# Keys and queries from two PSUM banks instead of three, the second product accumulated on a copy of the first

## The chip, the cores and the metric

The kernel runs on one core of one Trainium2 chip. The metric is the device time of one execution in microseconds (us); lower is better. The engines that matter are PE (the tensor engine, matmuls), ACT (the scalar engine), DVE (the vector engine), POOL, and SP, which issues most DMAs. Each engine works through its own list of instructions in order and waits at semaphores for the others.

## The reference

The input x has 2048 rows of 512 numbers. Cut to what matters:

```python
xn = layernorm(x)                                  # per row, eps 1e-5
# A: linear attention, 32 heads of 16
q, k, v = heads(xn @ wqkv)                         # per head, 2048 x 16
phi = lambda t: where(t > 0, t + 1, exp(t)) + 1e-6
num = phi(q) @ (phi(k).T @ v)
den = phi(q) @ phi(k).sum(rows) + 1e-6
s = concat_heads(num / den) @ wo
# B: token-mixing block, then an MLP
h  = gelu(layernorm(xn) @ w1)
x1 = xn + shift_rows(h, quarters of the columns by +1, -1, +2, -2) @ w2
g  = silu(x1 + gelu(layernorm(x1) @ w3) @ w4)      # 512 -> 1376 -> 512
out = x + s * g
```

## The kernel before

The 2048 rows are 16 tiles of 128, numbered 0 to 15, in four blocks of four tiles. A product of fp32 accuracy is made as three matmuls (`products`): each operand is split into a rounded high part and a low part, and high·high, high·low and low·high are added up in PSUM. A matmul of the kind that matters here is 128x512. The names in the profile and the order are those of the tiles with the buffer's number left out; `wk_0h` is the high part of a piece of the key weights, `u_0l` the low part of a piece of the rows.

PSUM holds eight banks: four of the pool `acc` (in the first part of the program they hold the Gram sums `g`), and four of the pool `mm`, which everything else takes in turn.

Keys and queries of block 0 are made directly (`k`, `q`; `qsum` is a row of column sums of the query weights, made from `wqmh`, which ACT rounds from `wqt`). For blocks 1 to 3 they are made by a scheme of seven products for a 2x2 block matrix: the left matrix is two row tiles (i and k = i+2) by two halves of the columns, the right one the key weights and the query weights by two halves of the rows. Seven products of sums replace eight. The sums of the rows are `U[b]` (a11, a12, a22, s1 to s4; in the trace `u` and `us`), those of the weights `TW` (b11, b21, b22, t1 to t4; in the trace `wk`, `kq`, `wq`). One call of `keys_queries(b, j)` makes the keys and queries of two tiles with 42 matmuls, six for each product. There are six calls, (1,0) to (3,1), with i = 4, 5, 8, 9, 12, 13.

In a call, PSUM banks `pbk`, `pek`, `pak` take the products; ACT copies a bank to SBUF with `pl.act(..., AF.Copy)`; DVE adds with `pl.tt(..., ALU.add)`. The key of tile i is a11·b11 + a12·b21: the first product stands in `pbk`, ACT copies it to `p1k`, the second is made in a bank of its own, `pak`, and DVE adds the two. The other three results need the running sums a11·b11 + s2·t2 (copied to `u2k`) and s1·t1 (copied to `p5k`). `feature_k` then applies phi with two ACT instructions (`kr`, `kt`) and goes on with DVE; `feature_q(i, t)` of these blocks stores the query t.

Behind this stage come `mix1`/`mix2` (tiles `h`, `pbm`, `pam`, `pem`), and from about 214 us on the MLP and the output of the attention of all four blocks (`a`, `pb`, `pe`, `pa`, `uc`, `pbs`, `pes`, `pas`). The last two groups of the program are the two column halves of tile 15, banks `a` and `a4x`, handled by `gate` (L1479). For `a`, DVE first adds a held part (`e<-a,e`), ACT applies silu (`th<-e`), DVE multiplies (`th<-th,so`) and adds x (`th<-th,xr`), and the result is stored. For `a4x` the held part is added by the tensor engine, and ACT reads the bank directly (`th<-a4x`).

What sets the order: the code only lists operations. `Plan.emit` is a list scheduler that walks time forward with modelled durations and picks on each engine the ready operation that is due first; a matmul that is later in the list may be drawn ahead to fill. A table of pairs, `SOONER` (an operation's number, and by how many quarters of a microsecond it is due sooner), nudges the due times by hand. The numbers count operations, so they shift when the code has more or fewer of them. On each engine the resulting list is then fixed.

Of the kernel before, what the change touches and what calls it, by code (L numbers as in the profile page):

```python
# [430 lines left out]
def linear_attn_gated_by_mixer(  # L431
# [479 lines left out]

    def keys_queries(b, j):

        i, k = b * QT + j, b * QT + j + 2
        pa, pb, pe = (bank(f"{n}k{i}") for n in ("pa", "pb", "pe"))
        p1, p5, u2 = (piece(f"{n}k{i}") for n in ("p1", "p5", "u2"))

        def go(ps, x, y, start=True):
            products(ps, [both(U[b][x][c], j * P, (j + 1) * P) + TW[y][c] for c in range(2)], start, more=not start)

        go(pb, "a11", "b11")
        pl.act(p1, pb, AF.Copy)
        go(pe, "s1", "t1")
        pl.act(p5, pe, AF.Copy)
        go(pb, "s2", "t2", False)
        pl.act(u2, pb, AF.Copy)
        go(pa, "a12", "b21")
        pl.tt(p1, pa, p1, ALU.add)
        go(pb, "s3", "t3", False)
        pl.tt(p5, pb, p5, ALU.add)  # L930
        go(pe, "s4", "b22", False)
        pl.tt(u2, u2, pe, ALU.add)
        feature_k(i, p1, True)
        go(pb, "a22", "t4", False)
        feature_k(k, pb, True)
        feature_q(i, u2)
        feature_q(k, p5)
# [727 lines left out]
    for b in range(NQ):  # L1665
# [138 lines left out]
```

## Time and profile before

| | |
|---|---|
| median of 3 runs | 503.85 us (503.77 to 504.27) |
| profiled execution | 503.29 us |
| its span | 501.5 us |
| granted clock, mean | 0.999 |

The span runs from the first to the last instruction on the core; 1.8 us of the time lie around it. The page gives busy shares per engine, the trace each instruction's start and duration. A matmul's duration (0.39 us for 128x512) is longer than the distance of two starts (0.23 us), since matmuls are pipelined.

| queue or engine | rows before |
|---|---|
| PE | 3102 instructions, 494.1 us busy |
| ACT | 859, 387.4 us |
| DVE | 944, 443.4 us |
| POOL | 97, 82.7 us |

### The profile page before, as it was taken

The numbers are of one execution on the slowest core, as the hardware profiler recorded it, in microseconds if no ns is written. First come the engines' busy times: TensorE is split into PE (matmuls) and PEld (weight loads), VectorE is DVE, ScalarE is ACT, GpSimd is POOL, SyncE is SP. The second block draws the span as 40 slices with busy tenths as digits, with TensorE's granted clock in tenths as the row PEclk, the third lists the DMA queues.
The fourth block names the chain that finished last, engine by engine and source line by source line (L and its number), as shares of the span: only waits on it lengthen the run. The fifth ranks groups of instructions, "written<-read, shape, count | busy, mean of one in ns | idle before, by whom it ended". The sixth has DMA issues, their size and how long they took to land.

```text
span 501.5 us, 9471 instructions
## 1 busy us (share of the span) xinstructions
PE 494.1 (99%) x3102; PEld 442.1 (88%) x3102; DVE 443.4 (88%) x944; ACT 387.4 (77%) x859; POOL 82.7 (16%) x97
## 2 busy tenths in 40 slices
PE   8999999999999999999999999999999999999996
PEld 6777887898888888899899999999899998999995
DVE  6899999999699896999999998998899979987364
ACT  6899799766888795977767688957799778977451
POOL 1267123131221022020100011200020200201101
PEclk9999999999999999999999999999999999999999
DMA  7959984479976799989776698988598886896805
GB/s 254 337 138 256 321 256 128 99 157 279 335 219 160 219 307 214 288 232 330 256 250 214 218 326 229 267 255 241 192 275 277 226 207 216 283 329 189 200 1 126
DMA packets 86989, 116.69 MB, mean 233 GB/s; under 512 B 8864, under 2 KB 41148, under 8 KB 86940
## 3 DMA queue, kind: packets, MB, share of 16 engines
q1 hardware_dynamic: 77004, 98.00, 60.2%
q0 software_dynamic: 9936, 18.09, 20.9%
q8 instruction: 24, 0.39, 0.3%
q14 instruction: 25, 0.20, 0.1%
HBM read 73.70 MB, written 32.91 MB: 213 GB/s over the span
## 4 chain that ended last, share of the span: by engine, by line
PE 90%; ACT 4%; DMA 3%; DVE 1%; SPq 0%; issue 0%; ACTq 0%
PE a L151 14%; PE pb L151 10%; PE h L151 9%; PE g L151 9%; PE pbk L151 7%; PE acc L151 6%; PE pe L151 5%; PE pbm L151 5%; PE pbs L151 5%; PE pek L151 3%; PE uc L151 3%; PE pa L151 2%; PE pes L151 2%; PE pem L151 2%; PE pak L151 2%; PE q L151 1%
## 5 line engine op out<-in xcount | busy, mean ns | idle before, releaser
L230 POOL DMA_DIRECT2D th<-in_x x14 | 12.3, 930 | 166.3 <-DMA w_t<-w4t 75.3
L230 POOL DMA_DIRECT2D o<-x x16 | 13.8, 866 | 63.9 <-DVE o L198 42.7
L178 ACT ACT_TABLE_LOAD x18 | 23.1, 1283 | 0.3
L230 POOL DMA_DIRECT2D zacc<-kr x16 | 16.9, 1058 | 35.6 <-DVE kr L208 16.8
L173 ACT ACTIVATE gf<-gf 128x256 f32<-128x256 f32 (+1 forms) x48 | 21.9, 468 | 0.3
L652 POOL TENSOR_TENSOR rs<-w,nhalf 128x4 f32<-128x4 f32 (+2 forms) x10 | 15.8, 1643 | 36.8 <-DVE w L203 36.8
L230 POOL DMA_DIRECT2D e<-x1d x12 | 10.6, 1083 | 63.3 <-DVE e L198 59.7
L173 ACT ACT_TABLE_LOAD x11 | 14.1, 1283 | 2.2 <-issue 1.0
L173 ACT ACTIVATE ht<-ht 128x512 f32<-128x512 f32 x16 | 9.8, 625 | 6.7 <-DVE ht L198 6.2
L208 DVE SCALAR_TENSOR_TENSOR kr<-kt,kr 128x512 f32<-128x512 f32 x16 | 10.9, 684 | 4.3 <-ACT kt L173 4.2
L198 DVE TENSOR_TENSOR th<-th,so 128x512 f32<-128x512 f32 (+1 forms) x17 | 11.0, 655 | 3.6 <-ACT th L173 3.6
L198 DVE TENSOR_TENSOR e<-a,e 128x512 f32<-128x512 f32 (+1 forms) x17 | 9.8, 588 | 4.8 <-PE a L151 4.8
L173 ACT ACTIVATE y<-o,nm,rs 128x512 f32<-128x512 f32 x16 | 11.8, 806 | 2.6 <-DVE nm L208 2.6
L646 DVE BATCH_NORM_STATS2 st<-o 128x6 f32<-128x512 f32 x16 | 10.8, 686 | 3.3 <-DMA o<-x 3.3
L173 ACT ACTIVATE p<-pe 128x256 f32<-128x256 f32 x20 | 7.6, 382 | 7.4 <-PE pe L151 7.4
L198 DVE TENSOR_TENSOR gf<-pa,p 128x256 f32<-128x256 f32 x20 | 8.4, 422 | 5.1 <-PE pa L151 4.5
L173 ACT ACTIVATE x<-x,nm,rs 128x512 f32<-128x512 f32 x16 | 12.9, 804 | 0.0
L173 ACT ACTIVATE th<-e 128x512 f32<-128x512 f32 (+1 forms) x12 | 7.1, 606 | 7.5 <-DVE e L198 7.4
L198 DVE TENSOR_TENSOR ht<-h,abc 128x512 f32<-128x512 f32 x16 | 10.9, 686 | 1.2 <-PE h L151 1.0
L173 ACT ACTIVATE p<-pb 128x256 f32<-128x256 f32 x20 | 7.5, 377 | 5.4 <-PE pb L151 5.3
L208 DVE SCALAR_TENSOR_TENSOR pq<-pq,rd 128x512 f32<-128x512 f32 x16 | 10.9, 678 | 0.1
L1413 DVE TENSOR_REDUCE den<-qz 128x32 f32<-128x512 f32 x16 | 10.8, 681 | 0.1
(1868 smaller groups left out, 2288.5 us busy)
## 6 DMA issues: line engine op xcount, KB each, us to landing
w_s<-in_w SPq DMA_DIRECT2D x34, 256.0 KB, 5.1
w_t<-w4t SPq DMA_DIRECT2D x26, 256.0 KB, 6.2
w_b<-w4d SPq DMA_DIRECT2D x24, 256.0 KB, 4.7
x<-in_x SPq DMA_DIRECT2D x16, 256.0 KB, 6.2
zacc<-kr POOLq DMA_DIRECT2D x16, 256.0 KB, 4.9
o<-x POOLq DMA_DIRECT2D x16, 256.0 KB, 4.7
x1d<-o SPq DMA_DIRECT2D x16, 256.0 KB, 3.2
xt<-in_xt SPq DMA_DIRECT2D x15, 256.0 KB, 6.3
```

Of the source, the lines that this page charges most:

```text
L151: lambda: nc.tensor.matmul(out.get(), lhs.get(), rhs.get(), start=start, stop=stop, skip_group_check=more))
L173: nc.scalar.activation(out.get(), src.get(), func, scale=get(scale), **kw)
L178: op.warm = lambda: nc.scalar.activation(self.scr[1].get(), self.scr[0].get(), func)
L198: self.vec(eng, out, [a, b], lambda: self.e(eng).tensor_tensor(out.get(), a.get(), b.get(), op=op), True)
L208: lambda: self.nc.vector.scalar_tensor_tensor(out.get(), a.get(), get(s), b.get(), op0=op0, op1=op1),
L230: lambda: self.nc.gpsimd.dma_start(out.get(), get(src), accum_op=ALU.add))
L646: pl.add("DVE", .62, .69, [xv], [st], lambda: nc.vector.bn_stats(st.get(), xv.get()))
L652: lambda: g.tensor_tensor(out.get(), src.get(), nh.get(), op=ALU.pow))
L1413: pl.add("DVE", .6, .68, [t], [den], lambda: nc.vector.tensor_reduce(den.get(), t.get().rearrange("p (h d) -> p h d", d=DH), axis=AX.X, op ...
```

## The change

The bank `pak` goes, and the tiles `p1k` and one meaning of `p5k` with it. After the first product, a11·b11, ACT copies its bank `pbk` into the bank `pek` (from PSUM to PSUM), and a12·b21 is accumulated there by the tensor engine with `start=False`. `pek` has held s1·t1 until then, so ACT must first have copied that to `p5k`. `feature_k` of tile i reads `pek` itself. Then ACT copies `pbk` (now a11·b11 + s2·t2) into `pek` a second time, for s4·b22 to be accumulated on it. DVE adds `p5k` to `pbk` and to `pek`, into the tiles `q2k` and `u2k`. Per call, three ACT copies stay three, and three DVE adds become two. The matmuls are the same 42. `seven_in_two` stood in the file before, called by nothing; the changed file has it twice, the same text.

```diff
+        go(pb, "a11", "b11", True)
+        go(pe, "s1", "t1", True)
+        pl.act(p5, pe, AF.Copy)
+        pl.act(pe, pb, AF.Copy)
+        go(pe, "a12", "b21", False)
+        go(pb, "s2", "t2", False)
+        first(pe)
+        pl.act(pe, pb, AF.Copy)
+        go(pb, "s3", "t3", False)
+        go(pe, "s4", "b22", False)
+        pl.tt(z2, pb, p5, ALU.add)
+        pl.tt(z1, pe, p5, ALU.add)
+        go(pb, "a22", "t4", False)
...
     def keys_queries(b, j):
 
         i, k = b * QT + j, b * QT + j + 2
-        pa, pb, pe = (bank(f"{n}k{i}") for n in ("pa", "pb", "pe"))
-        p1, p5, u2 = (piece(f"{n}k{i}") for n in ("p1", "p5", "u2"))
-
-        def go(ps, x, y, start=True):
+        pb, pe = (bank(f"{n}k{i}") for n in ("pb", "pe"))
+        p5, u2, q = (piece(f"{n}k{i}") for n in ("p5", "u2", "q2"))
+
+        def go(ps, x, y, start):
             products(ps, [both(U[b][x][c], j * P, (j + 1) * P) + TW[y][c] for c in range(2)], start, more=not start)
 
-        go(pb, "a11", "b11")
-        pl.act(p1, pb, AF.Copy)
-        go(pe, "s1", "t1")
-        pl.act(p5, pe, AF.Copy)
-        go(pb, "s2", "t2", False)
-        pl.act(u2, pb, AF.Copy)
-        go(pa, "a12", "b21")
-        pl.tt(p1, pa, p1, ALU.add)
-        go(pb, "s3", "t3", False)
-        pl.tt(p5, pb, p5, ALU.add)
-        go(pe, "s4", "b22", False)
-        pl.tt(u2, u2, pe, ALU.add)
-        feature_k(i, p1, True)
-        go(pb, "a22", "t4", False)
+        seven_in_two(go, pb, pe, p5, lambda v: feature_k(i, v, True), u2, q)
         feature_k(k, pb, True)
         feature_q(i, u2)
-        feature_q(k, p5)
+        feature_q(k, q)
...
     SOONER = (
-        0, 16, 2, 377, 19, 8894, 26, 3270, 31, 261, 34, 64, 36, 38809, 42, 3243, 43, 155, 55, 33, 62, 32, 72, 16,
...
+        2, 188, 19, 9650, 22, 64, 23, 48, 26, 3222, 31, 261, 36, 9687, 42, 3240, 43, 310, 58, 16, 62, 32, 70, 9,
...
```

The whole table is replaced, so the order changes on every engine and in all parts. The first place is call (1,0). On PE before, from the last a11·b11 matmul on, s1·t1 goes to `pek`, s2·t2 to `pbk`, and a12·b21 to a fresh bank:

```order
L151 MATMUL pbk_779<-wk_1h,u_1l 128x512 [waits DVE_49]
L151 MATMUL pek_803<-kq_0h,us_0h 128x512 [waits Activation_49]
L151 MATMUL pek_803<-kq_0l,us_0h 128x512 [waits DVE_49]
L151 MATMUL pek_803<-kq_0h,us_0l 128x512 [waits DVE_49]
L151 MATMUL pek_803<-kq_1h,us_0h 128x512
L151 MATMUL pek_803<-kq_1l,us_0h 128x512
L151 MATMUL pbk_779<-kq_0h,us_1h 128x512 [waits Activation_49]
L151 MATMUL pek_803<-kq_1h,us_0l 128x512
L151 MATMUL pbk_779<-kq_0l,us_1h 128x512 [waits DVE_49]
L151 MATMUL pbk_779<-kq_0h,us_1l 128x512 [waits DVE_49]
L151 MATMUL pbk_779<-kq_1h,us_1h 128x512
L151 MATMUL pbk_779<-kq_1l,us_1h 128x512 [waits DVE_49]
```

On PE now, from the last s1·t1 matmul on:

```order
L151 MATMUL pek_789<-kq_1h,us_0l 128x512
L151 MATMUL h_1_674<-u_3h,w_3h 128x512
L151 MATMUL h_1_674<-u_3l,w_3h 128x512
L151 MATMUL h_1_674<-u_3h,w_3l 128x512
L151 MATMUL pbk_772<-kq_0h,us_1h 128x512 [waits Activation_49]
L151 MATMUL pek_789<-wk_2h,u_2h 128x512
L151 MATMUL pek_789<-wk_2l,u_2h 128x512
L151 MATMUL pek_789<-wk_2h,u_2l 128x512 [waits DVE_49]
L151 MATMUL pek_789<-wk_3h,u_3h 128x512
```

Between the last s1·t1 matmul and the first that waits for ACT's copy (it overwrites `pbk`, which the copy reads) stand three matmuls of `h`; before, s2·t2 waited for a copy whose source is complete five matmuls earlier, and a12·b21 for none. ACT at the same place now has the two copies one behind the other, the second waiting for ACT's own first:

```order
L173 ACTIVATE p5k_818<-pek_789 128x512 [waits DMAHW6_49,PE_49]
L173 ACTIVATE pek_789<-pbk_772 128x512 [waits Activation_49]
L173 ACTIVATE kq_1h<-kq_1_822 128x512 [waits DVE_49]
L173 ACTIVATE us_3h<-us_3_831 128x512 [waits DVE_49]
L173 ACTIVATE kr_851<-pek_789,rs_93 128x512 [waits PE_49,Pool_49]
L173 ACTIVATE kt_861<-pek_789,rs_93 128x512
L173 ACTIVATE kq_1h<-kq_1_839 128x512 [waits DVE_49]
L173 ACTIVATE pek_789<-pbk_772 128x512 [waits PE_49,Activation_49]
```

The six calls differ in what stands between. Counted in PE's list of the changed kernel, with 0.232 us for a 128x512 matmul and 0.118 us for a 128x256 one:

| call | from the last s1·t1 matmul to the first that waits for the first copy | from the last a11·b11 | from the last s2·t2 to the first that waits for the second copy |
|---|---|---|---|
| (1,0) | 4 steps, 0.93 us | 2.32 us | 1.62 us |
| (1,1) | 6 steps, 1.39 us | 5.80 us | 1.73 us |
| (2,0) | 11 steps, 1.87 us | 0.59 us | 0.94 us |
| (2,1) | 20 steps, 3.73 us | 6.53 us | 1.62 us |
| (3,0) | 8 steps, 1.17 us | 0.70 us | 1.62 us |
| (3,1) | 4 steps, 0.93 us | 6.03 us | 1.87 us |

The second place is call (3,1) on ACT, where a `kr` of the call before stands between the two copies (`pek_2304` and `pbk_2257` are this call's banks, `pbk_2156` the earlier one's):

```order
L173 ACTIVATE k11h<-kr_1925 128x512 [waits DVE_49]
L173 ACTIVATE p5k_2314<-pek_2304 128x512 [waits DMASW7_49,PE_49]
L173 ACTIVATE kr_2331<-pbk_2156,rs_93 128x512 [waits DVE_49,PE_49]
L173 ACTIVATE pek_2304<-pbk_2257 128x512 [waits Activation_49]
L173 ACTIVATE kt_2338<-pbk_2156,rs_93 128x512 [waits DMAHW1_49]
L173 ACTIVATE k12h<-kr_2255 128x512
```

The `kr` there waits for the last matmul of a22·t4 of the earlier call, which PE has two rows behind this call's last s1·t1. In call (1,1), eight ACT instructions of other work (four `x`, four roundings) stand directly ahead of `p5k`; in (3,0), a load of an activation table stands between the first copy and `kt`, `kr`.

The third place is the head and the tail. On PE before, `qsum` stands behind four matmuls of this `q`:

```order
L151 MATMUL q_344<-wq_0h,u_0h 128x512 [waits DVE_49]
L151 MATMUL q_344<-wq_0l,u_0h 128x512
L151 MATMUL q_344<-wq_0h,u_0l 128x512
L151 MATMUL q_344<-wq_1h,u_1h 128x512
L151 MATMUL qsum<-wqmh,onesr 128x512 [waits DVE_49,Activation_49]
L151 MATMUL q_344<-wq_1l,u_1h 128x512
```

and now behind six:

```order
L151 MATMUL q_345<-wq_0h,u_0h 128x512 [waits DVE_49]
L151 MATMUL q_345<-wq_0l,u_0h 128x512
L151 MATMUL q_345<-wq_0h,u_0l 128x512
L151 MATMUL q_345<-wq_1h,u_1h 128x512
L151 MATMUL q_345<-wq_1l,u_1h 128x512
L151 MATMUL q_345<-wq_1h,u_1l 128x512
L151 MATMUL qsum<-wqmh,onesr 128x512 [waits DVE_49,Activation_49]
```

On DVE, the program ended before with the half that needs the add `e<-a,e`:

```order
L198 TENSOR_TENSOR th_0_7122<-th_0_7122,xr_6847 128x512 [waits DMAHW5_49,DVE_49]
L198 TENSOR_TENSOR th_256_7142<-th_256_7142,so_7058 128x256 [waits Activation_49]
L198 TENSOR_TENSOR th_256_7142<-th_256_7142,xr_6863 128x256 [waits DMAHW6_49,DVE_49]
L198 TENSOR_TENSOR e_6785<-a_3_6408,e_6785 128x256 [waits PE_49]
L198 TENSOR_TENSOR th_0_7158<-th_0_7158,so_7058 128x256 [waits Activation_49]
L198 TENSOR_TENSOR th_0_7158<-th_0_7158,xr_6863 128x256 [waits DVE_49]
```

and ends now with the half that ACT reads from the bank:

```order
L198 TENSOR_TENSOR e_6771<-a_3_6390,e_6771 128x256 [waits DMASW4_49,PE_49]
L198 TENSOR_TENSOR th_0_7109<-th_0_7109,xr_6865 128x512 [waits DMAHW5_49,DVE_49]
L198 TENSOR_TENSOR th_0_7129<-th_0_7129,so_7045 128x256 [waits Activation_49]
L198 TENSOR_TENSOR th_0_7129<-th_0_7129,xr_6876 128x256 [waits DMAHW6_49,DVE_49]
L198 TENSOR_TENSOR th_256_7145<-th_256_7145,so_7045 128x256 [waits Activation_49]
L198 TENSOR_TENSOR th_256_7145<-th_256_7145,xr_6876 128x256 [waits DVE_49]
```

On POOL, the memset of `ones`, for which PE's first matmul `warm` waits, has moved behind one `AFFINE_SELECT`. SP's list has one issue more (454 for 453 rows) in another order; early loads of the query weights stand ahead of some of x.

1 line of the change is left out of this document (added), and 34 rows, old and new, of the table SOONER.

## The prediction

> **What bounds the kernel now.** I read the busy times first, then what PE waited for, then windows cut at the calls of `keys_queries`, then the durations of the instructions that the change touches.
>
> ```profile
> PE 494.1 (99%) x3102; PEld 442.1 (88%) x3102; DVE 443.4 (88%) x944; ACT 387.4 (77%) x859; POOL 82.7 (16%) x97
> PE warm L151 <- POOL ones L548: 1.7, 1, 1.7
> PE qsum L151 <- ACT wqmh L173: 0.8, 1, 0.8
> 20.00:30.00 10.00, 9.18 (x41) 7.04 (x40) 9.61 (x27) 9.44 (x22) 4.72 (x7) 1.00 0.89 252
> 30.00:54.00 24.00, 24.00 (x106) 19.10 (x105) 23.59 (x46) 23.35 (x59) 14.17 (x12) 1.00 0.88 209
> 54.00:62.00 8.00, 8.00 (x36) 6.50 (x35) 8.00 (x15) 5.92 (x23) 1.76 (x2) 1.00 1.08 335
> 62.00:74.00 12.00, 12.00 (x54) 9.64 (x53) 11.76 (x25) 11.06 (x20) 2.27 (x2) 1.00 0.90 266
> 110.00:127.00 17.00, 17.00 (x102) 14.96 (x101) 16.43 (x41) 11.37 (x24) 3.64 (x4) 1.00 0.99 276
> 159.00:180.00 21.00, 21.00 (x101) 17.39 (x101) 19.45 (x42) 17.06 (x33) 2.59 (x3) 1.00 0.76 223
> 42.90 11.25 PE h L151 x48
> 68.06 1.38 PE pak L151 x6
> ```
>
> The first row is the page's busy time. The two rows below it are all that PE waited for in the whole span: its start, and once `qsum`. Then come windows (length, then busy us of PE, its weight loads, DVE, ACT, POOL, then the granted clock). In the four that hold five of the six calls PE is busy to the last hundredth, and DVE nearly so until 74 us. PE busy does not prove PE at its peak, since a matmul lasts longer than the distance of two starts; but the last two rows, pieces of the chain that ended last, have 48 matmuls of 128x512 in 11.25 us and 6 in 1.38, 0.234 and 0.230 each: nothing is lost between them. So PE's own list sets the time. DVE and ACT matter only where PE comes to wait for them, and less work on DVE is worth nothing by itself.
>
> **The change: the first copy.** Durations (min/median/max in ns) of what it takes out, puts in or stands beside:
>
> ```profile
> L173 ACT ACTIVATE p1k<-pbk x6: 577/600/602, 55.6 to 171.3; 128x512 f32<-128x512 f32 x6
> L173 ACT ACTIVATE p5k<-pek x6: 573/585/598, 57.5 to 174.6; 128x512 f32<-128x512 f32 x6
> L198 DVE TENSOR_TENSOR p1k<-pak,p1k x6: 682/686/692, 61.8 to 175.5; 128x512 f32<-128x512 f32 x6
> L151 PE MATMUL pek<-kq_1h,us_0l x6: 393/395/397, 56.8 to 172.3; 128*128 128x512 f32 x6
> L173 ACT ACTIVATE kq_1h<-kq x4: 615/624/633, 44.5 to 61.2; 128x512 fp32r<-128x512 f32 x4
> L173 ACT ACTIVATE kr<-pbk,rs x6: 674/685/690, 68.3 to 179.7; 128x512 f32<-128x512 f32 x6
> 55.16 0.40 PE L151 MATMUL pbk<-wk_1h,u_1l 128*128 128x512 f32 x1
> 55.59 0.60 ACT L173 ACTIVATE p1k<-pbk 128x512 f32<-128x512 f32 x1
> 67.60 0.80 ACT L173 ACTIVATE x<-x,nm,rs 128x512 f32<-128x512 f32 x1
> 68.30 0.68 ACT L173 ACTIVATE kr<-pbk,rs 128x512 f32<-128x512 f32 x1
> 68.87 0.68 ACT L173 ACTIVATE kt<-pbk,rs 128x512 f32<-128x512 f32 x1
> 21.58 0.39 PE L151 MATMUL q<-wq_1h,u_1h 128*128 128x512 f32 x1
> 22.12 0.62 ACT L173 ACTIVATE wqmh<-wqt 128x512 fp32r<-128x512 f32 x1
> 22.79 0.50 PE L151 MATMUL qsum<-wqmh,onesr 128*128 128x512 f32 x1 [0.82 <-ACT wqmh L173]
> 23.13 0.40 PE L151 MATMUL q<-wq_1l,u_1h 128*128 128x512 f32 x1
> 495.59 0.02 issue
> 1.66 0.29 POOL L551 TENSOR_SCALAR_AFFINE_SELECT ident<-ident 128x128 f32<-128x128 f32 x1
> ```
>
> Taken away: six DVE adds of 0.686, 4.1 us in all. They lie beside a PE that is never late for them, so they are worth 0. The three ACT copies per call stay three, and the matmuls stay 42. `kr` and `kt` of tile i now read PSUM (0.685, as those of tile k do), nothing on PE's path. The bank that is saved is worth 0 too: PE waits for no bank.
>
> Put in: a chain between two products. Before, a12·b21 went into a bank of its own. Now the bank is s1·t1's, and PE may go on only when ACT has copied s1·t1 out and a11·b11 in. A copy from PSUM to PSUM is not in the trace. The nearest rows are the copies from PSUM to SBUF (0.573 at the least) and from SBUF to SBUF (0.633 at the most). I take 0.60, the `p1k` row, which reads the same bank.
>
> From the start of the last s1·t1 matmul: 0.395 until it ends; 0.05 until ACT starts (55.16 + 0.40 to 55.59 is 0.03; 0.05 after `wqmh`'s end at 22.74 PE starts `qsum`); 0.585 for `p5k`; 0.02 for the hand-over from one copy to the next (the chain's `issue` row, between two engines); 0.60; 0.05 until PE starts. Sum 1.70 us. If only a11·b11 is late, it is 0.395 + 0.05 + 0.60 + 0.05 = 1.10. Behind the waiting matmul everything on PE is queued, so the chain less the matmuls between (counted in the table of calls) is lost time:
>
> - (1,0): 1.70 - 0.93 = 0.77.
> - (1,1): 1.70 - 1.39 = 0.31. Ahead of `p5k`, though, ACT has four `x` (0.70 to the next start: 67.60 to 68.30) and four roundings (0.62 less the 0.1 by which neighbours overlap), 4.9 us, against 18 matmuls and an end on PE meanwhile, 18 x 0.232 + 0.445 = 4.6. Of these 0.3 I take 0.2, since the copy before may end early. Taken 0.51.
> - (2,0): s1·t1 has 1.87 and is covered; a11·b11 ends late: 1.10 - 0.59 = 0.51.
> - (2,1): 3.73 covers all of it: 0. The cover is the matmuls between; without them it would be 0.77 like the others.
> - (3,0): 1.70 - 1.17 = 0.53.
> - (3,1): 1.70 - 0.93 = 0.77, and `kr` of the earlier call stands between the two copies: 0.57 more before the second can start. Taken 1.34.
>
> Sum of the first copies 3.66; without the two lateness terms of ACT, 2.89.
>
> **The second copy** waits for `kr` and `kt`, which read the bank, and for s2·t2. From the last s2·t2 matmul the chain is 1.10, against 1.62 in three calls, 1.73 and 1.87 in two, and 0.94 in (2,0), which makes 0.16 there. In the others it hangs on ACT's queue, the `kr` and `kt` at 0.685 with other work between; by these durations they come within 0.2 of PE. I take 0.4 for all six together, between 0.16 and 0.9.
>
> **The restart.** After its wait `qsum` starts at 22.79 and the next matmul at 23.13, 0.34 later instead of 0.23. So 0.1 for each wait, six to seven of them: 0.65. At the least it is 0.
>
> **The new order.** `qsum` now comes two matmuls later while ACT's way to `wqmh` is as long as before: 2 x 0.232 = -0.46 of its 0.82. The move of `ones` on POOL delays the first matmul by at most the 0.29 of an `AFFINE_SELECT`; what is left of the `qsum` wait takes that up, cost 0. SP's loads: PE waits for no load in the trace, so 0, and the `qsum` row is the size of what a late one would cost. At the end:
>
> ```profile
> 495.61 0.39 ACT L173 ACTIVATE th<-a4x 128x256 f32<-128x256 f32 x1 [1.25 <-PE a4x L151]
> 496.46 0.28 PE L151 MATMUL a<-w_9h,f_9l 128*128 128x256 f32 x1
> 496.83 0.42 DVE L198 TENSOR_TENSOR e<-a,e 128x256 f32<-128x256 f32 x1
> 497.28 0.42 ACT L173 ACTIVATE th<-e 128x256 f32<-128x256 f32 x1 [1.28 <-DVE e L198]
> 497.73 0.42 DVE L198 TENSOR_TENSOR th<-th,so 128x256 f32<-128x256 f32 x1 [0.48 <-ACT th L173]
> 481.78 0.70 PE pbs L151 x6
> 482.71 0.71 PE pes L151 x6
> 214.00:502.00 288.00, 282.64 (x2057) 266.24 (x2055) 249.61 (x532) 209.35 (x470) 27.69 (x31) 1.00 0.80 232
> ```
>
> After the last matmul come an add, silu, a multiply, an add and the store. With `a4x` last, ACT reads the bank itself, and the add of 0.42 with its 0.03 of hand-over goes: -0.45. SP's twelve stores of queries and POOL's gathers of `kr` stay, in number and kind, and no wait of PE names them: 0. The rest of the part after 214 us has the same work in a partly other order. Its PE gaps are the tail; smaller ones show only as groups of six that take 0.71 instead of 0.70. I take 0, and 0.8 either way for the range, the size of the one wait that the trace has.
>
> **Sum**: 3.66 + 0.4 + 0.65 - 0.46 - 0.45 = +3.8 us, on the profiled execution's 503.29: 507.1. The median of the runs stands 0.56 above that execution, so 507.6 for a median. The low end: 2.89 + 0.16 - 0.91 - 0.8 = +1.3, or 505.2. The high end: 3.66 + 0.9 + 0.65 + 0.8, without the gain at the head = +5.6, or 509.4.
>
> The Trainium skill, ScalarE: Activation LUTs, section "Step-by-step: what each stage is for", says that ScalarE reaches PSUM with less latency than SBUF, and Perfetto Trace Analysis, section "Optimizing Scalar/DVE Operations", puts the access overhead at about 51 against 93 ns. By that a copy would be 0.04 shorter, an estimate, and the five waits together 0.2: the sum would be +3.6. No row of this trace writes PSUM from ACT.
>
> **Rivals.**
>
> 1. The copies are covered: the matmuls between are enough, as before, where PE waits for none of the three. Then the order's 0.91 is left: 502.95. For it speaks that the fillers are there at all; it needs a copy of 0.2 us in (1,0) and (3,1), against a smallest row of 0.573.
> 2. The other side: the new order after 214 us wins more than the waits cost. Place: the 2057 matmuls there. Price: if each group of six (some 340) went from 0.71 to 0.70, 3.4 us. With the waits at their low end (3.05) and the head and tail: 503.85 + 3.05 - 0.91 - 3.4 = 502.6. It decides once that part gives back over 3.1 us at that low end. Against it, PE is busy for 282.64 of the 288, and the 5.4 left are the tail.
> 3. The waits last one pass, 1.10 instead of 1.70, because the two copies run into each other: 0.17 in (1,0), 0.51 in (2,0), 0.40 in (3,0) (1.10 - 0.70 from a11·b11), 0.74 in (3,1), 0.3 of restarts, less the order's 0.91: +1.2, or 505.05. Against it, the copy overwrites the bank that `p5k` reads, and waits for ACT's own semaphore.
> 4. ACT becomes the bound from 54 to 74 us: it is busy for 11.06 of 12, gets slightly longer `kr` and `kt` in a row, and each late instruction ahead of a copy is PE's wait. Twice the lateness terms (0.2 + 0.57) and 0.9 for the second copies are +1.3: 508.9, and with one more late `kr` in each of two calls 510.0. For it: DVE, which feeds ACT's roundings, is full there.
> 5. The clock falls. In the trace it stays at 1.00 in the window that holds the `qsum` wait. One call of 42 matmuls at twice the spacing would cost 42 x 0.23 = 9.7: 517.
>
> The Trainium skill, TensorE: Matmul & The Clock Gate, section "A second HAM failure mode: psum-queue depth-cycling", says that short idle times between groups, as banks are cycled, made the clock swing between half and full; that is rival 5. The `qsum` wait, the only row of such a length, does not show it.
>
> **How the numbers follow.** Forecast (505.2 to 509.4) 0.65; rival 1 0.06; rival 2 0.06; rival 3 0.08; rival 4 0.12; rival 5 0.03. About 0.2%, 1 us, is what a measurement of this kernel can tell from no change: 502.84 to 504.86 is the same. Rival 1 falls on its edge, half faster and half same; of rival 2 most (0.05) is faster; a third of rival 3 is the same. With 0.02 of the forecast's low end on either side: faster 0.10, same 0.09, slower 0.81. The range reaches down to 504.6, which takes in rival 3, and up to 509.6, which takes in half of rival 4.
>
> **What would show it.** Among PE's waits, rows of `pbk` or `pek` for ACT's `pek`, 3 to 5 us in all, longest about 1.3, in the call at about 170 us, and none in (2,1). PE below full in the windows of the calls, full between them. The `qsum` wait near 0.36. A chain that ends without `e<-a,e`. DVE 4.1 us less. Wrong it is if PE has no such rows, if a `pek<-pbk` copy lasts 0.3 us or less, or if the windows after 214 us differ by over 1 us.

## The result, and the profile after

| | median, us | range | runs |
|---|---|---|---|
| before | 504.06 | 503.77 to 504.31 | 4 |
| changed | 511.07 | 509.74 to 514.26 | 4 |

The ratio is 1.0149 (95% interval 1.0131 to 1.0168): slower by 7.0 us, where 3.8 were forecast, and above the range. The profiled execution is the slowest of the four, 514.26 us with a span of 512.3. In the page's busy times and in what PE waited for (total us, times, longest) it reads:

```profile
PE 498.2 (97%) x3102; PEld 443.8 (87%) x3102; DVE 438.6 (86%) x938; ACT 384.9 (75%) x856; POOL 79.4 (16%) x97
PE pbs L151 <- ACT p1s L173: 2.4, 1, 2.4
PE warm L151 <- POOL ones L548: 2.0, 1, 2.0
PE pek L151 <- ACT pek L173: 2.0, 4, 1.1
PE uc L151 <- DMA w_t<-w4t: 1.1, 2, 0.9
PE h L151 <- ACT w_1h L173: 0.7, 1, 0.7
PE pbk L151 <- ACT pek L173: 0.6, 1, 0.6
PE pes L151 <- DVE q4s0l L198: 0.2, 1, 0.2
```

The `pek` and `pbk` rows are the forecast ones. The rows of `pbs`, `uc` and `h` were not forecast, and behind each of them stands a transfer, as is shown further down. The same windows as before:

```profile
20.00:30.00 10.00, 10.00 (x45) 7.69 (x43) 9.65 (x27) 9.64 (x24) 4.69 (x7) 1.00 0.93 279
30.00:54.00 24.00, 23.18 (x100) 18.00 (x99) 22.80 (x45) 22.65 (x56) 10.90 (x12) 1.00 0.89 211
54.00:62.00 8.00, 7.39 (x33) 5.69 (x32) 8.00 (x16) 7.04 (x27) 1.75 (x2) 1.00 1.05 313
62.00:74.00 12.00, 11.79 (x51) 8.95 (x50) 11.51 (x25) 11.38 (x21) 2.27 (x2) 1.00 1.06 328
110.00:127.00 17.00, 16.61 (x97) 14.35 (x96) 16.20 (x38) 9.23 (x22) 5.39 (x6) 1.00 1.01 273
159.00:180.00 21.00, 19.57 (x99) 16.04 (x98) 15.38 (x31) 16.63 (x43) 2.73 (x4) 1.00 0.71 179
214.00:502.00 288.00, 284.18 (x2058) 268.01 (x2057) 250.57 (x537) 215.18 (x480) 27.23 (x30) 0.99 0.80 231
```

The calls' windows lose 0.61, 0.21, 0.39 and 1.43 us at a clock of 1.00, while the `qsum` loss at 20 to 30 us is gone. But 30:54, full before, also loses 0.82, and the long window has a clock below 1.00. The copies, as rows of one tile each (min/median/max in ns):

```profile
L173 ACT ACTIVATE pek<-pbk x12: 571/582/622, 57.5 to 181.9; 128x512 f32<-128x512 f32 x12
L173 ACT ACTIVATE p5k<-pek x6: 582/598/602, 56.9 to 176.6; 128x512 f32<-128x512 f32 x6
L151 PE MATMUL pek<-wk_2h,u_2h x6: 392/496/498, 58.5 to 178.3; 128*128 128x512 f32 x6
```

A copy within PSUM takes 0.582, against 0.60 assumed. The last row is the matmul that in four of the six calls waits for the first copy: 0.496 at the median instead of 0.395 (the `pek` row of the trace before), which is the restart. In call (1,0) a matmul of `pbk` waits instead, and in (2,1) none does. Call (3,1), the longest wait, in order of time:

```profile
176.14 0.40 PE L151 MATMUL pek<-kq_1h,us_0l 128*128 128x512 f32 x1
176.58 0.60 ACT L173 ACTIVATE p5k<-pek 128x512 f32<-128x512 f32 x1 [2.91 <-PE pek L151]
177.07 0.68 ACT L173 ACTIVATE kr<-pbk,rs 128x512 f32<-128x512 f32 x1
177.64 0.60 ACT L173 ACTIVATE pek<-pbk 128x512 f32<-128x512 f32 x1
178.29 0.50 PE L151 MATMUL pek<-wk_2h,u_2h 128*128 128x512 f32 x1 [1.06 <-ACT pek L173]
```

From 176.14 to 178.29 are 2.15; the forecast was 1.70 and 0.57 for `kr`, 2.27.

**Where the time went.** Waits do not add up all that is lost, so I took, over all matmuls, the distance of two starts less the usual one of that width (0.232 us for 512, 0.118 for 256, the medians of the trace before), and summed by stretch. `first` is the start of PE's first matmul, `end` the time from its last start to the end of the span:

| kernel | first | 0-30 us | 30-50 | 50-192 | 192-340 | 340-390 | 390-425 | 425 on | end |
|---|---|---|---|---|---|---|---|---|---|
| before | 1.67 | 4.58 | 0.15 | 0.03 | 0.86 | 0.80 | 0.15 | 0.55 | 5.02 |
| changed | 2.05 | 3.55 | 1.39 | 5.07 | 0.27 | 0.75 | 6.21 | 0.39 | 4.98 |
| `after_again` | 2.05 | 4.25 | 1.46 | 4.94 | 0.30 | 1.84 | 0.81 | 0.38 | 5.36 |
| `order_alone` | 2.05 | 3.54 | 1.44 | 1.08 | 3.74 | 0.69 | 3.23 | 1.44 | 4.69 |
| `new_first_old_second` | 2.05 | 3.49 | 1.49 | 5.46 | 1.26 | 0.78 | 0.05 | 0.42 | 5.00 |
| `copy_before_kr` | 2.05 | 4.11 | 1.46 | 4.57 | 1.11 | 0.83 | 0.07 | 0.41 | 5.00 |
| `calls_only` | 1.67 | 4.20 | 0.16 | 4.96 | 2.04 | 0.86 | 0.11 | 0.49 | 5.02 |
| `head_only` | 2.05 | 4.42 | 1.47 | 0.80 | 0.67 | 0.86 | 0.11 | 0.40 | 5.03 |
| `old_to_289` | 1.67 | 4.84 | 0.23 | 0.01 | 2.10 | 0.20 | 1.76 | 0.38 | 4.50 |
| `tail_new` | 1.67 | 4.95 | 0.19 | 0.02 | 0.84 | 0.81 | 0.10 | 0.59 | 4.51 |

Each row is one profiled execution; the lower rows are the experiments below. Stretches repeat to 0.1 or 0.2 where a kernel keeps its order, with two exceptions: 0-30 moves by a microsecond from run to run, and 50-192 of the two-bank order by 0.9, since a wait at `pam` for `ha122h` (near 158 us, not one of the copies) comes in some executions and not in others. For the changed kernel the stretch of the calls costs 5.0, which the forecast's 4.7 (3.66 + 0.4 + 0.65) nearly covers; 0.5 of it is that wait. The rest of the miss lies in the head (0-50), behind 340 us and at the end.

### The profile page after: what moved, and what is told of

It reads as the page before. It is cut to its first block, busy times and chain, and to the rows that moved or that the text cites. A ratio compares the mean times of both kernels' runs of the same rounds, so it can differ in the third digit from the quotient of the medians.

```text
span 512.3 us, 9461 instructions
## 1 busy us (share of the span) xinstructions
PE 498.2 (97%) x3102; PEld 443.8 (87%) x3102; DVE 438.6 (86%) x938; ACT 384.9 (75%) x856; POOL 79.4 (16%) x97
## 4 chain that ended last, share of the span: by engine, by line
PE 83%; DMA 8%; ACT 3%; DVE 2%; issue 1%; SPq 0%; POOL 0%; DVEq 0%; ACTq 0%; POOLq 0%
PE a L151 13%; PE pb L151 10%; PE h L151 7%; PE g L151 7%; PE acc L151 6%; PE pbk L151 5%; PE pe L151 5%; PE pbs L151 4%; PE pek L151 4%; PE pbm L151 4%; PE pa L151 3%; PE uc L151 2%; PE k L151 2%; PE pem L151 2%; PE pes L151 2%; DMA q10d<-q10z 2%
## 5 line engine op out<-in xcount | busy, mean ns | idle before, releaser
L652 POOL TENSOR_TENSOR rs<-w,nhalf 128x4 f32<-128x4 f32 (+2 forms) x10 | 13.6, 1361 | 41.1 <-DVE w L203 32.8
L173 ACT ACTIVATE e<-uc 128x256 f32<-128x256 f32 x24 | 7.6, 384 | 5.3 <-PE uc L151 5.3
L208 DVE SCALAR_TENSOR_TENSOR qz<-pq,zb 128x512 f32<-128x512 f32 x16 | 10.9, 683 | 0.0
```

Source lines behind the costliest of these rows:

```text
L173: nc.scalar.activation(out.get(), src.get(), func, scale=get(scale), **kw)
L208: lambda: self.nc.vector.scalar_tensor_tensor(out.get(), a.get(), get(s), b.get(), op0=op0, op1=op1),
L652: lambda: g.tensor_tensor(out.get(), src.get(), nh.get(), op=ALU.pow))
```

## The experiments

**The theories after the result.** A: the two banks cost what was forecast, 4 to 5 us, and the remainder comes from the new order, in waits for transfers that the trace before could not show as PE's. Rival B: the two banks cost more than PE's waits show, for example by a lower clock or late work handed on to later stages; then the new order with three banks is no slower than before. A third account, C in the expectations: the second part loses because it starts late, whatever its order. The first four kernels tried to part scheme and order with the code's own planner.

**`after_again`**, the changed kernel once more, with no edit, for the scatter.

> The changed kernel once more, with a profile of its own. Theory A (two banks cost what their waits cost, about 4.5 us between 30 and 214 us; the rest of the loss is waits of the second part, after 214 us, that hang on when a transfer lands and so differ from run to run): the five waits for the first copy come again as 0.77, 0.36, 0.53, 0.53, 1.23 within 0.05, while the waits at 397 and 412 us (0.9 for `w_t`, 2.4 for `p1s`, followed by 3.4 us at half clock) change in size or are gone; time 509.5 to 512. Theory B (the loss of the second part is a fixed consequence of the order): the waits at 397 and 412 us come again within 0.1, time 511 to 514. Theory C (the two banks delay everything behind them, and the transfers of the second part collide because it starts later): as B.

It took 512.23 (510.87 to 516.07), ratio 1.0195 (1.0148 to 1.0242): +8.7, just above the range of theory A. The waits in the calls are the same to 0.01 us (0.768, 0.366, 0.530, 0.180, 0.521 and 1.225). The `pbs` wait at 412 us, which with the slow stretch behind it cost 4.3 us of the profiled execution above, is absent. So the calls are fixed, and what varies lies behind 340 us.

**`scheme_old_order`**, two banks, with the old nudges under the new numbers:

```diff
     SOONER = (
-        2, 188, 19, 9650, 22, 64, 23, 48, 26, 3222, 31, 261, 36, 9687, 42, 3240, 43, 310, 58, 16, 62, 32, 70, 9,
+        0, 16, 2, 377, 19, 8894, 26, 3270, 31, 261, 34, 64, 36, 38809, 42, 3243, 43, 155, 55, 33,
...
```

> The changed kernel with the old table of nudges, carried over operation by operation: two banks without the new order. In PE's list only 0.23 us lie between the last s1t1 matmul and the first that waits in four calls, 0.46 in (3,1), 1.39 in (1,1), so by the chain of 1.70 us the first copies cost 1.47 x 4 + 1.24 + 0.31 = 7.4 us, with second copies of 0.5 and restarts of 0.1 each about 8.9. Theory A: waits of these sizes, PE's idle in the windows of the calls about 7.9 in all, the second part as in the kernel before or 1 us worse: 512 to 514. Theory C: the second part starts 9 us later and collides worse than in the changed kernel: 516 or more. Rival (the new order costs everything, the two banks nothing): 504 to 505.

It took 542.96 (542.16 to 544.84), ratio 1.0786 (1.0764 to 1.0808), 30 us over the expectation. What PE waited for:

```profile
PE pek L151 <- ACT pek L173: 6.7, 5, 1.9
PE a L151 <- ACT f_0sh L173: 5.6, 1, 5.6
PE a L151 <- ACT f_1a L173: 2.8, 1, 2.8
...
PE pbk L151 <- ACT pek L173: 1.3, 1, 1.3
```

The copies lose more when the order isn't made for them, 8.0 in the two rows of `pek` and `pbk`. By the distances of starts the calls' stretch (50 to 192 us) loses 16.0, and there, after the wait of 1.9, the granted clock was 0.50 for 3.4 us. Behind 192 us lie another 27.9: the nudges of the second part hang on operations whose neighbours have changed. As a test of the scheme it says little.

**`order_alone`**, three banks, the new nudges under the old numbers.

```diff
-        2, 188, 19, 9650, ... 582, 26, 599, 8, 617, -4, 618, 4, 627, -13, 631, 13, 636, 92,
+        2, 188, 19, 9650, ... 582, 26, 593, 8, 612, -4, 614, 4, 628, -13, 632, 13, 637, 92,
...
-        seven_in_two(go, pb, pe, p5, lambda v: feature_k(i, v, True), u2, q)
+        go(pa, "a12", "b21")
+        pl.tt(p1, pa, p1, ALU.add)
```

> The kernel before, three banks, with the new table carried over operation by operation. Theory A: no wait in the six calls; the head gains about 0.7 at `qsum` and loses about 1.3 at `h` (the wait for `w_1h` at 43 us), the end of the last chain 0.45 earlier; the second part as far as its order is that of the changed kernel costs 1 to 3 us: 504.5 to 507. Theory C: nothing but head and tail, 504 to 504.8. Rival (the new order costs everything): 510 to 511.

It took 512.2 (510.05 to 513.56), ratio 1.0166 (1.0136 to 1.0196). The windows of the calls are full where the changed kernel's are not:

```profile
54.00:62.00 8.00, 8.00 (x36) 6.49 (x35) 8.00 (x16) 7.03 (x27) 1.75 (x2) 1.00 1.07 339
62.00:74.00 12.00, 12.00 (x54) 9.61 (x53) 11.72 (x25) 10.91 (x19) 2.26 (x2) 1.00 0.94 297
159.00:180.00 21.00, 21.00 (x105) 17.61 (x105) 14.98 (x31) 14.20 (x35) 1.73 (x2) 1.00 0.74 198
```

So the waits of `pek` and `pbk` belong to the two banks, and the head's 1.44 at 30 to 50 us to the order. The time as a whole was missed, since the planner made another second part than the changed kernel has.

**`new_then_old`**, two banks, the new nudges up to 190 us and the old ones behind.

```diff
-        1786, 32, 1967, 64, 1986, 32, 2204, -16, 2286, 32, 2318, -16, 2479, 9, 2530, 32, 2551, 16, 2839, -84,
+        1786, 32, 1935, -8, 1940, -8, 2190, 16, 2225, 8, 2272, 5, 2286, 32, 2479, 9, 2489, -8, 2511, -5,
...
```

> The changed kernel with the new table up to the start of the second part (about 190 us), and the old one, carried over, from there. In it `q8s1l`, which in the changed kernel waits for a store that reads the buffer it gets, waits for no transfer. Theory A: the first part as in the changed kernel (waits for the copies 3.6 us, `h` 1.2), and the second part close to that of the kernel before: 508.5 to 510, with runs closer together than the 4.5 us of the changed kernel. Theory C: the second part is as late, so it loses the same: 510 to 514.

It took 534.87 (533.86 to 535.2), ratio 1.0617 (1.0601 to 1.0632). The calls' stretch lost 4.54, close to the changed kernel's 5.07 and 4.94, and the second part shows the waits of 5.6, 3.3, 2.8 and 2.6 of the old nudges. Nudges do not carry over. From here on the kernels issue recorded lists, with the recorded buffers, instead of planning:

```diff
-    def emit(self, first, lead, reserve, window, ahead, table=()):
-        self.deadlines(first)
-        self.nudged(table)
+    def emit(self, table):
+        for word in table.split():
+            word, _, chosen = word.partition(":")
+            op, chosen = self.ops[int(word.rstrip("w"))], [int(c) for c in chosen.split(",") if c]
...
-            ahead=6.0, table=SOONER)
+    pl.emit(ORDERED)
```

Lists of the two kernels can be joined where both have done the same work, at 192 us.

**`new_first_old_second`**, two banks:

```diff
-all operations as in the kernel before
+operations up to 192 us as in the changed kernel, the others as in the kernel before
```

> Two banks, with every engine's list and every buffer exactly as in the changed kernel up to about 192 us, and exactly as in the kernel before from there (the two lists hold the same work at that point, but for one operation). Theory A (the second part's new order and buffers cost what is lost beyond the first part): the first part loses what the profile of the changed kernel shows there, 10.4 us over the bare matmuls against 4.7, so +5.7; the second part loses no more than before (2.2): 509 to 509.5, runs within 1 us of each other. Theory C (the second part loses because it starts later, whatever its order): 510.5 to 513, and PE waits for `uc` or `pbs` again.

It took 510.03 (508.87 to 510.53), ratio 1.012 (1.0106 to 1.0134): +6.2. What PE waited for:

```profile
PE pek L151 <- ACT pek L173: 2.0, 4, 1.1
PE h L151 <- ACT w_1h L173: 0.7, 1, 0.7
PE pbk L151 <- ACT pek L173: 0.6, 1, 0.6
PE pam L151 <- ACT ha122h L173: 0.4, 1, 0.4
```

The time lies between the ranges of the two theories, half a microsecond above that of A, but the table decides: nearly all of the loss is in the first part, and from 340 us on, though PE comes there about 6 us later, it loses 0.78, 0.05 and 0.42, as the kernel before. That speaks against C. Of the 5.46 in the calls' stretch the `pam` wait, which is not one of the copies, is 0.4, and 0.9 by distances of starts with the three slow starts behind it.

**`old_first_new_second`**, three banks, joined the other way at 192 us:

```diff
-operations after 192 us as in the kernel before
+operations after 192 us as in the changed kernel
```

> The other half: three banks and the lists of the kernel before up to about 192 us, then the lists and buffers of the changed kernel. Theory A: no wait in the calls; the second part loses 2 to 4 us more than before, with waits for `w_t` near 390 us and, in some runs, of `pbs` near 402 us: 505.5 to 508, with runs over 1 us apart. Theory C: 503.5 to 504.5.

It took 512.34 (511.16 to 513.69), ratio 1.0178 (1.0157 to 1.02), above both expectations. That is no measure of the second part: 6.9 us are lost right behind the joint, where PE waits 3.3 us for `ha123h` and then runs at a granted clock of 0.50 for 6.8 us. `old_to_289` repeats it with a better joint.

**`copy_before_kr`**: as `new_first_old_second`, but ACT's second copy of call (3,1) goes ahead of the earlier call's `kr`.

```diff
 L173 ACTIVATE p5k_2314<-pek_2304 128x512
-L173 ACTIVATE kr_2331<-pbk_2156,rs_93 128x512
 L173 ACTIVATE pek_2304<-pbk_2257 128x512
+L173 ACTIVATE kr_2332<-pbk_2156,rs_93 128x512
```

> As the first of these (new first part, old second part), with one change: in call (3,1) ACT makes the copy of a11b11 into the bank directly behind `p5k`, and `kr` of the earlier call only then. If the wait there is the chain of two copies plus one `kr` between them (1.23 measured), it falls by about 0.57, to 0.66, and the time by as much, 508.5 to 509. If the wait is set by PE's side or by the copies alone, it stays at 1.23.

It took 509.25 (508.92 to 509.38), ratio 1.0107 (1.0093 to 1.0121), inside the other's interval. The timeline at the same place:

```profile
176.70 0.60 ACT L173 ACTIVATE p5k<-pek 128x512 f32<-128x512 f32 x1 [2.93 <-PE pek L151]
177.33 0.58 ACT L173 ACTIVATE pek<-pbk 128x512 f32<-128x512 f32 x1
177.96 0.50 PE L151 MATMUL pek<-wk_2h,u_2h 128*128 128x512 f32 x1 [0.61 <-ACT pek L173]
...
182.85 0.50 PE L151 MATMUL pbk<-kq_0h,us_2h 128*128 128x512 f32 x1 [0.20 <-ACT pek L173]
```

Measured by distances of starts, the wait falls from 1.225 to 0.773, which is the chain of 1.70 less 0.93 to the hundredth. Of the 0.45 won, 0.36 come back at 182.85, with another restart of 0.1: `kr` is later, so is the second copy, and PE waits for that one. So the move wins nothing; that the stretch is 0.89 shorter in the table is the `pam` wait, which this execution doesn't have.

**`qsum_later`**, three banks, the kernel before with one step moved:

```diff
 L151 MATMUL q_344<-wq_1h,u_1h 128x512
-L151 MATMUL qsum<-wqmh,onesr 128x512
 L151 MATMUL q_344<-wq_1l,u_1h 128x512
 L151 MATMUL q_344<-wq_1h,u_1l 128x512
 L151 MATMUL q_344<-wq_2h,u_2h 128x512
 L151 MATMUL q_344<-wq_2l,u_2h 128x512
+L151 MATMUL qsum<-wqmh,onesr 128x512
```

> The kernel before, with one matmul moved: the first of `qsum` four matmuls later on PE, all else the same. If its wait of 0.82 (0.97 with the restart) is time lost, the wait goes and the time falls by about 0.9 us, to 502.6 to 503.2. If what PE loses there comes back behind it (another engine or a transfer sets the time of the head), it stays at 503.5.

It took 503.36 (502.56 to 504.16, 11 runs), ratio 0.999 (0.9981 to 0.9999): -0.5, just told from zero and half of what was expected. In the profiled execution the wait of 0.8 is gone, but `k` waits 0.4 for `wk_0h` at the start and `qsum` 0.2 for `wqml`.

**`old_to_289`**, three banks, old order up to 289 us, new order behind:

```diff
-operations after 289 us as in the kernel before
+operations after 289 us as in the changed kernel
```

> Three banks, every list and buffer as in the kernel before up to about 289 us, and as in the changed kernel from there; the two lists hold the same work at that point but for one operation, and each engine is in the middle of the same stage, so there should be no wait at the joint as there was at 211 us. Theory A (the new second part has waits of its own): PE waits for `pes` near 335 us (0.4 to 1.4) and for `uc` on `w_t` near 390 us (0.7 to 1.3), in some runs for `pbs` near 405; 505 to 507, scattered by over 1 us. Theory C (it loses only because it starts late): none of these, 503.5 to 504.5.

It took 505.16 (503.81 to 510.06, 10 runs), ratio 1.004 (1.0018 to 1.0062): +1.5 with the tail's gain in it. The chain behind its longest wait, as timeline rows:

```profile
383.35 0.68 DVE L198 TENSOR_TENSOR w_1l<-w_fb,w_1h 128x512 fp32r<-128x512 f32 x1
384.28 0.38 SPq L222 DMA_DIRECT2D w4t<-w_1l  x1
388.80 2.74 SPq L226 DMA_DIRECT2D w_t<-w4t  x4
394.88 0.50 PE L151 MATMUL uc<-w_t,f_2th 128*128 128x256 f32 x2 [1.52 <-DMA w_t<-w4t]
```

DVE makes a piece of the weights, SP stores it, loads it back transposed, and PE needs it. In the kernel before, `w_1l` is made at 365.8 and stored at 366.5, 17.6 us earlier; the store landed 9.4 us later and nobody waited.

**`old_289_early_w1l`**, the same with `w_1l` and its store ahead of their neighbours:

```diff
 L198 TENSOR_TENSOR sf_1a<-gf_6_5354,sf_1b 128x256
+L198 TENSOR_TENSOR w_2_1l<-w_2_fb,w_2_1h 128x512
...
 L198 TENSOR_TENSOR f_1tl<-sf_1b,f_1th 128x512
-L198 TENSOR_TENSOR w_2_1l<-w_2_fb,w_2_1h 128x512
```

> The same with four instructions moved forward: DVE makes `w_1l` five instructions earlier, SP stores it to `w4t` six issues earlier, and SP issues the two loads of `w_t` that read it ahead of the store of `th` (buffers exchanged so that each has one free). If the wait of `uc` near 390 us is the chain `w_1l` to store to load (DVE makes it at 389 us in the changed kernel, at 366 in the kernel before), the wait is gone and 0.7 to 1.2 us with it; if the transfers are late for lack of bandwidth, the wait stays.

It took 509.58 (508.74 to 510.41), ratio 1.0118 (1.0101 to 1.0136), slower by 4.4 than without the move. PE's longest waits, and the moved step:

```profile
PE pb L151 <- DVE gf L198: 3.3, 1, 3.3
PE uc L151 <- DMA w_t<-w4t: 0.3, 1, 0.3
383.77 0.69 DVE L198 TENSOR_TENSOR w_1l<-w_fb,w_1h 128x512 fp32r<-128x512 f32 x1 [4.33 <-DMA out<-th]
```

The buffer that `w_1l` writes was still being read by a store, DVE stood 4.33 us, and PE behind it 3.3. So `w_1l` came no earlier (383.77 against 383.35), nor did its store (384.49 against 384.28), and the step could not be earlier at that place in this order. The `uc` wait fell from 1.5 to 0.3, but PE came to that matmul 3.0 us later (397.92 against 394.88), so this does not test the chain: it is read from the rows above, not shown by a change.

**`tail_new`**, three banks, the kernel before with the last two groups exchanged:

```diff
+L151 MATMUL a_3_6408<-w_3_3h,f_3l 128x256
...
+L151 MATMUL a_3_6408<-w_3_9h,f_9l 128x256
 L151 MATMUL a4x<-xi,identr 128x256 x2
...
-L151 MATMUL a_3_6408<-w_3_3h,f_3l 128x256
...
-L151 MATMUL a_3_6408<-w_3_9h,f_9l 128x256
```

> The kernel before with the last 20 us in the changed kernel's order: `a` before `a4x`, nothing else moved. My prediction said -0.45: then 503.1 to 503.4. By the traces of the changed order the last add ends 0.45 earlier after the last matmul, but the last store lands 3.1 to 3.8 us after it instead of 2.87, since it is issued behind two others within 1.3 us: then no gain, 503.5 to 504.2.

It took 503.25 (502.67 to 503.69, 11 runs), ratio 0.9988 (0.9979 to 0.9997): -0.4. The time from the last matmul to the end fell from 5.02 to 4.51, the forecast 0.45 with the store's own scatter.

**`calls_only`**, two banks, the new order from 48 to 192 us alone:

```diff
-operations from 48 to 192 us as in the kernel before
+operations from 48 to 192 us as in the changed kernel
```

> Two banks in the changed kernel's order from about 48 to 192 us only; the lists and buffers before and behind are those of the kernel before. If the loss of the first part is the waits for the copies (3.4 first, 0.2 second, 0.1 of restart each), with the one of `pam` for `ha122h` (0.2 to 0.8) and a little at the joint at 192 us, it is 4.5 to 5.3: 508.2 to 509. If the late start of `warm` and the waits of `h` at 43 us matter for it, which are left out here, it is under 4: 507 or less.

It took 509.62 (509.32 to 510.32), ratio 1.0121 (1.0108 to 1.0135): +6.1. In the table it loses 4.96 in the calls' stretch, against 0.03, and 1.2 more behind the joint at 192 us, in three late starts of `pbm` and `pem` with their restarts (`pem` waits 0.2 for ACT's copy `p5m`). The time is 0.6 above the expectation. Its clock is 1.00 throughout. This speaks against B's clock; that the stage hands late work on is seen here, but in a joint that the changed kernel doesn't have.

**`head_only`**, three banks, the new order up to 48 us alone:

```diff
-operations up to 48 us as in the kernel before
+operations up to 48 us as in the changed kernel
```

> Three banks in the changed kernel's order up to about 48 us only, the rest as in the kernel before. My prediction put -0.46 here. By the traces PE's first matmul is 0.38 late, `qsum` no longer waits, and `h` waits 1.2 to 1.4 for `w_1h` and `w_2h`, which land when they did before: +0.3 to +1.2, 504 to 505.

It took 505.43 (504.55 to 507.19, 7 runs), ratio 1.004 (1.0024 to 1.0056): +1.9, a little above the expectation; 0.7 of it lie behind the joint (50-192 in the table). The rows of `h`, first of the kernel before, then of this one:

```profile
43.23 0.63 ACT L173 ACTIVATE w_1h<-w_s 128x512 fp32r<-128x512 f32 x1 [0.45 <-DMA w_s<-w1t]
43.91 0.19 PEld L151 LDWEIGHTS h<-u_1h,w_1h 128*128 128x128 f32 x1 [0.28 <-ACT w_1h L173]
43.92 0.49 PE L151 MATMUL h<-u_1h,w_1h 128*128 128x512 f32 x1
```

```profile
44.25 0.63 ACT L173 ACTIVATE w_1h<-w_s 128x512 fp32r<-128x512 f32 x1 [0.89 <-DMA w_s<-w1t]
44.93 0.49 PE L151 MATMUL h<-u_1h,w_1h 128*128 128x512 f32 x1 [0.65 <-ACT w_1h L173]
```

Before, ACT already waits 0.45 for the transfer of `w_s` and the weight load 0.28 for ACT: PE gets its weights just in time, with nothing to spare. From the first matmul of `h` (five of 0.232 stand ahead of `w_1h`'s) to the start of `w_1h` on ACT are 0.39 to 0.57 in all nine profiles with the old head, which is what PE can bear, and 1.30 to 1.38 in all seven with the new one. The transfer that ACT waits for is the third of `w_s<-w1t`. With the new head POOL issues it 5.95 us ahead of the first matmul of `h` (with the old one 6.21 to 6.24), and it takes 7.2 to 7.3 us (6.6 to 6.8), in all of these profiles. In the changed kernel PE comes to `h` at 42.08 instead of 42.74, and `w_1h` starts at 43.46 instead of 43.23.

**`qsum_and_tail`**, three banks, the kernel before with the moves of `qsum_later` and `tail_new` together.

> The kernel before with both small moves that gained alone: `qsum` four matmuls later (0.5 measured) and `a` ahead of `a4x` at the end (0.4 to 0.6 measured). If they add up, 1.0 us: 502.4 to 502.9, faster than both kernels.

It took 503.06 (502.64 to 503.65, 11 runs), ratio 0.9987 (0.9978 to 0.9996): -0.5, not the sum of the two. It beats both kernels, the one before by 0.04 to 0.22%; of the whole change this much is worth keeping.

## Why the prediction was wrong in size

The sign and the mechanism held; the time did not. By its own terms, in us:

| term | forecast | shown |
|---|---|---|
| first copies | 3.66 | 3.42 |
| second copies | 0.4 | 0.2 |
| restarts | 0.65 | 0.7 |
| head (`qsum`, `ones`) | -0.46 | about +0.9 |
| second part (192 us on) | 0 ± 0.8 | +1.0 (`after_again`), +2.1 (`old_to_289`) and +5.3 (the changed kernel's profile) |
| tail | -0.45 | -0.5 alone (`tail_new`); 0.0 and +0.3 in the changed kernel |

**The copies were right**, call by call, from the distances of starts in the changed kernel: (1,0) 0.77 forecast, 0.768 measured; (1,1) 0.51 and 0.363; (2,0) 0.51 and 0.530; (2,1) 0 and 0; (3,0) 0.53 and 0.531; (3,1) 1.34 and 1.225. The chain of 1.70 against the matmuls between is thus right to 0.01 or 0.02 where nothing else stands on ACT. Some luck is in the last hundredth: in (1,0) `p5k` took 0.60 and `pek<-pbk` 0.58, the other way round from the 0.585 and 0.60 in the sum. The two lateness terms were a little high, since in (1,1) ACT caught up and in (3,1) `kr` cost 0.45 instead of 0.57. Of the second copies that of (2,0) showed, 0.179 against the 0.16 worked out, and that of (1,0) with 0.06. The seven restarts, one behind each of these waits, cost 0.10 each. These three terms make 4.3 of the 5.07 in the calls' stretch; 0.5 of the rest is the `pam` wait with its slow starts, which the prediction did not have. Rival 1 (all covered), 3 (one pass) and 4 (ACT as the bound) are excluded by these rows. The Trainium skill's figure for PSUM in Perfetto Trace Analysis, section "Optimizing Scalar/DVE Operations", would have made a copy 0.04 shorter, an estimate; measured, 0.582 within PSUM stands to 0.585 (`p5k` before), 0.598 (`p5k` now) and 0.600 (`p1k` before) from PSUM to SBUF, so 0.003 to 0.018.

**The failed step is "The new order"**, in two of its sentences.

"What is left of the `qsum` wait takes that up, cost 0", and the credit of 0.46. The 0-30 stretch of the seven profiled executions with the new head loses 3.96 on average (3.49 to 4.42), that of nine with the old head 4.77 (4.20 to 5.18). So 0.8 are won there: in the changed kernel's profile the `qsum` wait went altogether. But the first matmul starts 0.38 later, not the 0.29 at most of the prediction, and 1.3 are lost at 30 to 50 us, at `h`. In sum +0.9. It is not that PE comes to `h` too early: in `head_only` it comes at 42.95, 0.2 later than before, and loses the 1.3 all the same. The transfer of `w_s` had no slack, and in the new order it lands about 0.8 later as seen from PE. Why it takes half a microsecond longer was not tried. The row with `[0.45 <-DMA w_s<-w1t]` on ACT stood in the trace before; I had read PE's waits alone.

"SP's loads: PE waits for no load in the trace, so 0" and "I take 0, and 0.8 either way". That PE waits for none says that each came early enough in the old order, not by how much. In the new one `w_1l` comes at 387.35 instead of 365.8, and PE waits 0.9 for `w_t`, in `old_to_289` (383.35) 1.5. A bound drawn from the one wait in the trace was too small for 2057 reordered matmuls. How large it can be is seen at 412 us of the changed kernel's profile. In the chain that ended last, then in the timeline:

```profile
395.99 7.41 DMA w_10l<-w4d
403.46 9.36 DMA q10d<-q10z
412.91 0.69 DVE q8s1l L198
412.91 0.69 DVE L198 TENSOR_TENSOR q8s1l<-q8f,q8s1h 128x512 fp32r<-128x512 f32 x1 [4.06 <-DMA q10d<-q10z]
414.92 0.39 PE L151 MATMUL pbs<-m_t2h,q8s0h 128*128 128x256 f32 x1 [2.42 <-ACT p1s L173]
416.71 0.41 PE L151 MATMUL pbs<-m_t3h,q8s1h 128*128 128x256 f32 x1
```

A load took 7.41 us, the store of `q10z` behind it 9.36, DVE's next buffer was free only then, ACT waited for DVE and PE for ACT. In `after_again` the same order had no such wait: there the store is issued at 403.49, 0.03 later than here, but the load that needs it can be issued at 409.02 instead of 412.87, and `q8s1l` starts at 409.82, after a wait of 0.42 for ACT. Instructions and order being the same, what differs is when the transfers land. The 10 runs of `old_to_289` scatter over 6 us for the same reason, it seems; only one of them has a profile. Their two slowest, 507.16 and 510.06, have a mean clock of 0.996, as the changed kernel's slowest has.

The misses are 1.4 for the head, 0.3 for the calls' stretch, about 0.5 for the tail and 1.0 to 5.3 for the second part, 3.2 to 7.5 together; the single runs of the first measurement missed by 2.1 to 6.7, their median by 3.5. The prediction's own sign of being wrong, windows after 214 us that differ by over 1 us, is there. Theory A holds as far as the sum goes: the kernel with the new first part is at +6.2, the one with the new part after 289 us at +1.5, together 7.7 against 7.0 measured (interval 6.6 to 8.5) and 8.7 in `after_again`. Of B and of rival 5, the clock did fall, but in the second part and not in the calls; there it fell in `scheme_old_order` alone, behind its wait of 1.85. Rival 2 is excluded: the second part lost.

**Left open.** Why `pes` waits at 342 us (by distances of starts 1.4 in `after_again`, 0.4 in the changed kernel's first profile) was not tried. That the second part loses by late transfers is read from the traces for `uc` and `pbs`; no run took only one of these waits away. Nor was the stretch from 192 to 289 us measured alone. In the two profiles of the changed kernel the tail's gain is there up to the issue of the last store (1.6 us after the start of the last matmul as in `tail_new`, against 2.2 before), but from this issue to the end of the span are 3.34 and 3.72, against 2.86 in `tail_new` and 2.84 before; the cause was not tried.

## What to carry to other kernels

Where a saved bank puts two copies in a row between two products, count the chain (here 1.70 us) against the matmuls from the last that the first copy reads to the one that waits, some eight of 0.232, and look at what else ACT has queued between the two copies. A step that no engine waits for is not free to move: before crediting or ignoring a new order, read also what ACT, DVE and the weight loads wait for, and how early each transfer lands that PE uses next. Hand-made nudges belong to one list of operations; two kernels that carried the old ones over to a slightly different list came out 31 and 39 us slower than the one before, a third that carried over the new ones 9 us.

## What the hardware showed unexpectedly

After the wait of 2.42 us at 414.92, matmuls of 256 columns ran 0.118 apart for 1.4 us, and then from 416.5 to 419.7 they took 0.41 instead of 0.28 and were 0.21 apart, at a granted clock of 0.50. Other profiles show the same: `old_289_early_w1l` for 3.4 us behind its wait of 3.3, `old_first_new_second` for 6.8 us behind its wait of 3.3, and `scheme_old_order` for 3.4 us (175.7 to 179.1) behind one of 1.85. Once the clock had come up after the start, PE's waits of up to 1.5 us did not do it in any profile. The Trainium skill, TensorE: Matmul & The Clock Gate, section "What's actually happening", lets the clock fall after an idle window of about 3.4 us; here waits of 2.42 and 1.85 us were enough, and in three of these four places the slow stretch lasted about as long as that window. A copy inside PSUM by ACT, into a bank that matmuls had written just before, followed by matmuls that accumulate on it, works at the price of an ordinary copy (0.582 against 0.585 to 0.600).
